# Casting loads, states on both row halves and a new instruction order in the first batches of an attention and feed-forward kernel

## The chip, the cores and the metric

The kernel runs on one core of a Trainium2 chip. The metric is device time in microseconds of one execution, the median of several runs. The engines have queues of their own and run side by side: TensorE (PE in the profile, with its weight loads as PEld), VectorE (DVE), ScalarE (ACT), Pool (POOL) and SyncE (SP, which only issues transfers here). Each engine takes its instructions in order.

## The reference

```python
B, H, S, Ns, D = 8, 8, 512, 32, 64            # x (B,H,S,D), state (B,H,Ns,D), fp32
scores  = x @ state^T / sqrt(D)               # rows: 512 tokens, over 32 states
xread   = softmax(scores) @ state
scores2 = state @ x^T / sqrt(D)               # rows: 32 states, over 512 tokens
sread   = softmax(scores2) @ x
z = concat([xread, sread], axis=2)            # (B, H, 544, D)
z = z.transpose(0, 2, 1, 3).reshape(4352, 512)
h = z @ w_in                                  # (512, 2048)
out = max(0.01 * h, h) @ w_out                # (2048, 512)
```

## The kernel before, in words

The work goes batch by batch. For the 512 token rows of a batch, `xread @ w_in` is taken as probabilities times (state @ w_in): `a_m` (L364) makes a batch's matrix M = state @ w_in in four column blocks of 512, each in two PSUM banks of 128 rows (4 heads of 32 states each), and `m_evict` (L384) casts it to bf16. `ff1` (L394) multiplies 128 columns of M with the probabilities `aT`, two matmuls of 512 columns, and ScalarE evicts the product with the leaky relu into `hT`; `ff1_pair` does two at a time. The second product, `hT` times `w_out`, is done for batch 0 in pieces of one matmul each (`piece`, L602) and for the other batches in a form with seven products instead of eight (`Batch`, L697; a unit is two matmuls of 256 columns, `Fast.unit`, L670). That form needs sums of quarters of `w_out` (`weights_sum`, L638, into the `tw` tiles) and of `hT` (`Fast.sums`, L657).

The attention of a batch: `a_scores` (L212) makes the scores of all heads in the PSUM tile "sc"; `a_shift` takes the maximum over the 32 states on VectorE, spreads it, subtracts it; `a_exp` on ScalarE; `a_probs` sums, inverts, spreads and multiplies into `aT`. `a_max2`, `a_exp2` and `a_probs2` do the softmax over tokens for the state rows, whose read (`a_sread_rows`, L335, and for the last batch `a_sread`, L320) comes later, after a transpose by DMA (`a_a2t`).

Batch 0 has an order of its own: its tokens come in four transfers, TensorE transposes them, and its ff1 is done in quads (`Quad`, L942: eight matmuls of 256 columns, over half the tokens). Ten spins of TensorE on a zero tile stand at the start (`spin`, L139).

The loads: `w_in` and `w_out` are cast to bf16 by transfers from Pool's queue, in the order of the program (L881, L903 to L912): w_in's four quarters, w_out's first quarter, batch 1's x in two halves as fp32 (`x1`), w_out's second quarter in two parts, its third, batch 2's x as fp32 (`xl`), w_out's fourth in two parts. From batch 3 on, SyncE loads x as fp32 (`load_x`, L105). The fp32 tokens are cast into `xb` by VectorE for batch 1, by ScalarE and Pool for batch 2 and by Pool after that (`cast_x`, L112). `a_xt_dma` (L199) then transposes them by DMA from SyncE's queue; batch 1's are transposed by TensorE (L1014). The states of batches 0 and 1 are transposed by matmuls (`state01`, L156), those of batches 2 to 3 and 4 to 7 by Pool's cast and a DMA transpose (`state_t`, L185). A state head lies on row half g (64 rows) for an even or odd head.

The order is written out by hand: every engine's instructions follow the program (`manual_schedule`), and PSUM tiles of one tag ("ph" and "py" with two banks each in turn, "sc" and "big" with one of two banks) are passed on when their last reader is done. Lines 976 to 1118 are the order of batches 0 and 1; the loop at L1122 does batches 2 to 7 with a list of how many units go beside each ff1 (`PACE`, and `PACE2` for batch 2). The tail (L1250 on) does the state rows.

Of the kernel before, what the change touches and what calls it, by code (L numbers as in the profile page):

```python
# [9 lines left out]
P = 128  # L10
B, H, S, D = 8, 8, 512, 64
NS = 32
# [18 lines left out]
def kernel(  # L31
# [41 lines left out]
    idle = consts.tile([P, S], BF16, name="idle")  # L73
# [6 lines left out]
    identg = consts.tile([P, 2, P - NS], BF16, name="identg")  # L80
    nc.gpsimd.memset(identg[:], 0.0)
    heads = ident[:].rearrange("p (b k v q) -> p b k v q", b=2, k=NK, v=2)
    for g in range(2):
        for u in range(2):
            nc.gpsimd.tensor_copy(
                identg[:, g, :D].rearrange("p (k v q) -> p k v q", k=NK, v=2)[:, 2 * u:2 * u + 2, g ^ u],
                heads[:, 0, 2 * u:2 * u + 2, g],
            )
        nc.gpsimd.tensor_copy(
            identg[:, g, D:].rearrange("p (k q) -> p k q", k=NK), heads[:, 1, :, g]  # L90
        )
# [11 lines left out]
    xs, xl = {}, {}  # L103

    def load_x(b, eng):  # L105
        xl[b] = xpool.tile([P, H, NT * D], FP32, name="xl", tag="xl", bufs=1)
        eng.dma_start(xl[b][:], x[b].rearrange("h (p t) d -> p h (t d)", t=NT))

    def open_xb(b):
        xs[b] = xpool.tile([P, NT, H, D], BF16, name="xb", tag="xb")  # L110

    def cast_x(b, h0, h1, copy):  # L112
        copy(  # L113
            xs[b][:, :, h0:h1].rearrange("p t h d -> p h t d"),
            xl[b][:, h0:h1].rearrange("p h (t d) -> p h t d", t=NT),
        )

# [13 lines left out]
    def load_w_out(c, parts=1):  # L131
        n = 4 // parts
        for j in range(4 * c, 4 * (c + 1), n):
            nc.gpsimd.dma_start(
                w_out_bf[:, j:j + n, :],
                moe_w_out[P * j:P * (j + n), :].rearrange("(j p) f -> p j f", p=P),
            )
# [9 lines left out]
    st1 = consts.tile([P, P], BF16, name="st1")  # L147
    groups = ((2, 4), (4, 8))
    st_t = [consts.tile([P, hi - lo, P], BF16, name=f"st_t{lo}") for lo, hi in groups]
# [4 lines left out]
    stb0 = consts.tile([P, 4, D], BF16, name="stb0")  # L154

    def state01():  # L156
        ps = psum.tile([P, 4, P - NS], FP32, name="pst0", tag="big", bufs=1)
        for r in range(4):
# [10 lines left out]
            st1[:].rearrange("p (k q r) -> p k q r", k=NK, r=4),  # L169
            ps[:, :, D:].rearrange("p r (k q) -> p k q r", q=8),  # L170
# [3 lines left out]
    stb = [consts.tile([P, hi - lo, P], BF16, name=f"stb{lo}") for lo, hi in groups]  # L174
# [10 lines left out]
    def state_t(i):  # L185
        POO(stb[i][:], stf[i][:])
        nc.sync.dma_start_transpose(st_t[i][:], stb[i][:].rearrange("p b q -> p (b q)"))

# [3 lines left out]
    def a_open(a, b):  # L194
        a.b = b
        a.xb = xs[b]
        a.xT = att.tile([P, NT, NK, P], BF16, name="xT", tag="xT")

    def a_xt_dma(a):  # L199
        nc.sync.dma_start_transpose(  # L200
            a.xT[:].rearrange("p t k q -> p (t k) q"),
            a.xb[:].rearrange("p t h d -> p (t h d)"),
        )

    def st_of(a, g, k):
        rows = slice(D * g, D * (g + 1))
# [3 lines left out]
        return t[rows, NS * k:NS * (k + 1)]  # L210

    def a_scores(a):  # L212
        sc = psum.tile([P, 2, S], FP32, name="sc", tag="sc", bufs=1)
        for k in range(NK):
            for g in range(2):
                nc.tensor.matmul(  # L216
                    sc[NS * k:NS * (k + 1), g, :],
                    lhsT=st_of(a, g, k),
                    rhs=a.xT[D * g:D * (g + 1), :, k, :],
                    start=True, stop=True,  # L220
                )
        a.sc = sc

# [37 lines left out]
    def block_probs(dst, e1, q1h, n):  # L261
        q1b = att.tile([P, n, NS], BF16, name="qb", tag="qb", bufs=1)
        nc.vector.transpose(q1b[:], q1h[:, :, None].to_broadcast([P, n, NS]))
        nc.vector.tensor_tensor(  # L264
# [4 lines left out]
    def a_shift(a, part=None):  # L269
        flat = a.sc[:].rearrange("p g c -> p (g c)")  # L270
        if part != 1:
            a.mb = block_rows(block_max(flat, NB), NB)
        if part != 0:
            a.sh = block_sub(flat, a.mb, NB)
# [4 lines left out]
    def a_probs(a, part=None):  # L279
        if part != 1:  # L280
            a.q1h = block_recip(a.e1, NB)
        if part != 0:
            a.aT = att.tile([P, 2, S], BF16, name="aT", tag="aT")
            block_probs(a.aT[:], a.e1, a.q1h, NB)

    def a_max2(a):
        m2 = att.tile([P, 2], FP32, name="mcol", tag="mcol")
        nc.vector.tensor_reduce(out=m2[:], in_=a.sc[:], axis=AX.X, op=ALU.max, negate=True)  # L288
# [3 lines left out]
    def a_exp2(a, g):  # L292
        if g == 0:
# [3 lines left out]
            out=a.e2[:, g], in_=a.sc[:, g, :], func=AF.Exp,  # L297
# [22 lines left out]
    def a_sread(a):  # L320
        ps = psum.tile([P, NK, 2, NS], FP32, name="psr", tag="big", bufs=1)
        for k in range(NK):
            for i in range(NT):
                nc.tensor.matmul(
                    ps[:, k, :, :],
                    lhsT=a.xb[:, i, 2 * k:2 * k + 2, :].rearrange("p h d -> p (h d)"),
                    rhs=a.a2T[:, :, i, NS * k:NS * (k + 1)],
                    start=(i == 0), stop=(i == NT - 1),
                )
        for g in range(2):  # L330
            nc.scalar.copy(
                sr_t[D * g:D * (g + 1), a.b], ps[D * g:D * (g + 1), :, g, :],
            )
# [1002 lines left out]
```

## Time and profile before

| | |
|---|---|
| time, median of 3 runs | 202.02 us (201.66 to 202.12) |
| profiled execution, from first to last instruction | 199.8 us, 4974 instructions |
| what the timed median lies above that span | 2.2 us |
| granted TensorE clock | 1.00 throughout |
| TensorE / VectorE / ScalarE / Pool busy | 97% / 80% / 72% / 28% |
| DMA, mean over the span | 140 GB/s, 28.01 MB |

How to read it: a timeline row has start and length in us, engine, line, operation, tiles written<-read, shapes and count; what stands in brackets is the idle time just before it and what ended it. In a group row, "busy, mean ns of one" follow the bar, then idle time and its cause. A matmul's length holds its way through the array: the distance between starts is what it costs when others follow. In the transfers' part the last figure is the median time from issue to landing.

### The profile page before, as it was taken

Reading aid. Unit: us, or ns where it says so; the run is one execution under the profiler, and the core shown is the slowest. Engines: PE = TensorE matmul, PEld = TensorE weight load, DVE = VectorE, ACT = ScalarE, POOL = GpSimd, SP = SyncE. Lnnn points to the kernel's source line nnn. Section 1 sums busy time; section 2 is a strip of 40 time slices with the busy share of each in tenths; the row PEclk is TensorE's granted clock in tenths of the full one; section 3 lists DMA queues with packets and bytes.
Section 4 is the critical chain, followed back from the end, with each engine's and each line's share of the span. In section 5 each row is a group of like instructions: output and inputs, shape, how many; then the busy total and the mean of one; then the engine's idle time right before and its main releaser. Section 6 shows DMA issues by size and latency. Waiting matters only on the chain.

```text
span 199.8 us, 4974 instructions
## 1 busy us (share of the span) xinstructions
PE 193.2 (97%) x2044; PEld 134.3 (67%) x2066; DVE 160.8 (80%) x249; ACT 143.5 (72%) x263; POOL 55.4 (28%) x82
## 2 busy tenths in 40 slices
PE   7999999999999999999999999999999999999993
PEld 2566633446676767766776677667767788799882
DVE  2676689999999989966997499879978977995622
ACT  3478748599877867877797859787878768767710
POOL 8483174690027004200320041100020024005250
PEclk9999999999999999999999999999999999999999
DMA  5999997999581993269414945290025102210035
GB/s 195 221 206 271 236 296 137 221 286 202 112 223 28 302 266 73 47 213 272 91 24 195 241 43 107 105 164 0 0 108 157 30 0 94 119 56 0 0 95 171
DMA packets 39510, 28.01 MB, mean 140 GB/s; under 512 B 25344, under 2 KB 36736, under 8 KB 39488
## 3 DMA queue, kind: packets, MB, share of 16 engines
q1 hardware_dynamic: 33712, 20.35, 40.8%
q0 software_dynamic: 4944, 6.55, 16.0%
q10 hardware_dynamic: 832, 0.79, 1.2%
q8 instruction: 16, 0.26, 0.5%
q14 instruction: 6, 0.05, 0.1%
HBM read 17.30 MB, written 8.91 MB: 131 GB/s over the span
## 4 chain that ended last, share of the span: by engine, by line
PE 96%; DVE 1%; issue 1%; ACT 1%
PE yq L679 44%; PE ph L397 20%; PE pm L376 4%; PE py L608 4%; PE pyw L608 4%; PE pf L475 3%; PE yu L679 3%; PE ph L958 3%; PE pspin L142 2%; PE pl L564 2%; PE sc L216 1%; PE psn L342 1%; PE php L958 1%; PE phw L410 1%; PE scn L826 1%
## 5 line engine op out<-in xcount | busy, mean ns | idle before, releaser
L403 ACT ACTIVATE hT<-ph 128x512 bf16<-128x512 f32 x100 | 58.5, 605 | 18.4 <-PE ph L397 11.9
L679 PEld LDWEIGHTS <-su 128*128 128x128 bf16 x480 | 45.9, 98 | 14.8 <-DVE su L668 0.8
L397 PE MATMUL ph<-aT,M 128*128 128x512 bf16 x180 | 54.4, 379 | 0.3
L679 PEld LDWEIGHTS <-hT 128*128 128x128 bf16 x336 | 32.3, 98 | 14.3 <-issue 2.5
L679 PE MATMUL yq<-tw_xf,su 128*128 128x256 bf16 x224 | 31.6, 273 | 0.3
L679 PE MATMUL yq<-w_out_bf,hT 128*128 128x256 bf16 x224 | 31.0, 273 | 0.1
L113 POOL CAST xb<-xl 128x512 bf16<-128x512 f32 (+1 forms) x24 | 13.9, 621 | 49.9 <-DMA xl<-in_x_dram 36.7
L668 DVE TENSOR_TENSOR su<-hT 128x1024 bf16<-128x1024 bf16 (+1 forms) x27 | 19.3, 718 | 6.7 <-ACT hT L403 6.7
L397 PEld LDWEIGHTS <-M 128*128 128x128 bf16 x200 | 19.5, 98 | 5.7 <-DVE aT L264 0.2
L751 POOL TENSOR_TENSOR yo<-sv,sv 128x512 f32<-128x512 f32 x7 | 9.1, 1295 | 39.2 <-ACT sv L688 19.4
L688 ACT COPY sv<-yq 128x512 f32<-128x512 f32 x28 | 16.3, 586 | 3.0 <-PE yq L679 2.5
L679 PE MATMUL yq<-w_out_bf,su 128*128 128x256 bf16 x112 | 15.3, 273 | 0.3
L679 PE MATMUL yq<-tw_x,su 128*128 128x256 bf16 x112 | 15.5, 273 | 0.0
L691 DVE TENSOR_TENSOR yo<-yq,sv 128x512 f32<-128x512 f32 x20 | 13.6, 681 | 1.5 <-PE yq L679 1.5
L679 PE MATMUL yq<-tw_x,hT 128*128 128x256 bf16 x104 | 14.5, 273 | 0.0
L390 ACT CAST M<-pm 128x1024 bf16<-128x1024 f32 x12 | 12.2, 1018 | 0.2 <-PE pm L376 0.2
L296 ACT ACTIVATE e<-sc,mcols 128x512 bf16<-128x512 f32 x16 | 11.0, 695 | 0.6 <-DVE mcols L290 0.6
L608 PEld LDWEIGHTS <-hT 128*128 128x128 bf16 x64 | 5.9, 98 | 7.0 <-issue 1.1
L668 DVE TENSOR_TENSOR su<-su,hT 128x1024 bf16<-128x1024 bf16 x14 | 9.7, 692 | 0.5
L288 DVE TENSOR_REDUCE mcol<-sc 128x2 f32<-128x1024 f32 x8 | 9.7, 1214 | 0.0
L226 DVE TRANSPOSE_TENSOR_REDUCE mrow<-sc 128x32 f32<-128x1024 f32 x7 | 8.7, 1240 | 0.5 <-PE sc L216 0.5
L668 DVE TENSOR_TENSOR su<-hT,su 128x2048 bf16<-128x2048 bf16 (+1 forms) x8 | 9.1, 1132 | 0.0
(173 smaller groups left out, 302.6 us busy)
## 6 DMA issues: line engine op xcount, KB each, us to landing
out_dram<-yo SPq DMA_DIRECT2D x12, 512.0 KB, 2.7
xl<-in_x_dram SPq DMA_DIRECT2D x5, 1024.0 KB, 6.7
w_in_bf<-in_moe_w_in_dram POOLq DMA_DIRECT2D x4, 512.0 KB, 7.8
w_out_bf<-in_moe_w_out_dram POOLq DMA_DIRECT2D x2, 512.0 KB, 12.9
x<-in_x_dram POOLq DMA_DIRECT2D x2, 512.0 KB, 11.5
w_out_bf<-in_moe_w_out_dram POOLq DMA_DIRECT2D x4, 256.0 KB, 13.7
xl<-in_x_dram POOLq DMA_DIRECT2D x1, 1024.0 KB, 16.4
out_dram<-ysb SPq DMA_DIRECT2D x4, 256.0 KB, 5.6
```

The source lines that it names most:

```text
L113: copy(xs[b][:, :, h0:h1].rearrange("p t h d -> p h t d"), xl[b][:, h0:h1].rearrange("p h (t d) -> p h t d", t=NT),)
L288: nc.vector.tensor_reduce(out=m2[:], in_=a.sc[:], axis=AX.X, op=ALU.max, negate=True)
L296: nc.scalar.activation(out=a.e2[:, g], in_=a.sc[:, g, :], func=AF.Exp, bias=a.m2s[:, g:g + 1], scale=SCALE, accum_out=a.r2[:, g:g + 1],)
L390: copy(a.M[:, :, cols], pm[:])
L397: nc.tensor.matmul(ph[:], lhsT=a.M[:, g, P * j:P * (j + 1)], rhs=a.aT[:, g, :], start=(g == 0), stop=(g == 1),)
L403: nc.scalar.activation(out=hT[:, j, :], in_=ph[:], func=AF.Prelu, alpha=0.01)
L608: nc.tensor.matmul(y.py, lhsT=hT[:, j, P * i:P * (i + 1)], rhs=w_out_bf[:, j, :], start=(j == 0), stop=(j == 15),)
L668: (eng or nc.vector).tensor_tensor(out=S[n][:, ms], in0=u[:, ms], in1=v[:, ms], op=op)
L679: nc.tensor.matmul(bank[:, i, :], lhsT=lhs[:, m, P * i:P * (i + 1)], rhs=rhs[:, m, :], start=(first and m == 0 and (i == 0 or of is not No ...
L688: copy(t[:], bank)
L691: nc.vector.tensor_tensor(out=dst, in0=bank, in1=self.sv[n][:], op=ALU.add)
L751: nc.gpsimd.tensor_tensor(out=self.yo(1)[:, :, HC:], in0=f.sv[7][:], in1=f.sv[5][:], op=ALU.add)
```

## The change

Tokens of batches 1 to 7 are loaded as bf16 by casting transfers from Pool's queue, in halves for batches 1 and 2, and there is no cast of x by an engine any more. The layout of `xb` becomes head by head, so that a transpose of 128 columns holds two of a head's four token groups: a head's tokens lie on both row halves of `xT`. So the states are put on both row halves too (`state01` and the state transposes get twice as wide, `state_cast` makes two copies), and the scores of a batch become sixteen matmuls of 256 columns instead of eight of 512. The output rows are numbered accordingly. `a_sread` of the last batch becomes 32 matmuls of 64 rows for 16 of 128. The loads from Pool go in the order w_in, x of batch 1, three quarters of w_out, x of batch 2, the last quarter. Two of `w_out`'s sums that VectorE made are Pool's. The order of everything from the second quad to the end of batch 2's stretch is new, and written out call by call: which evictions go to VectorE or ScalarE, which PSUM tile a product takes, and where the pieces, ff1 products and units stand. The loop now runs over batches 3 to 7.

```diff
-    xs, xl = {}, {}
-    def load_x(b, eng):
-        xl[b] = xpool.tile([P, H, NT * D], FP32, name="xl", tag="xl", bufs=1)
-        eng.dma_start(xl[b][:], x[b].rearrange("h (p t) d -> p h (t d)", t=NT))
+    def load_x(b, h0=0, h1=H):
+        nc.gpsimd.dma_start(
+            xs[b][:, h0:h1].rearrange("p h t d -> p h (t d)"),
+            x[b, h0:h1].rearrange("h (p t) d -> p h (t d)", t=NT),
+        )
...
-        ps = psum.tile([P, 4, P - NS], FP32, name="pst0", tag="big", bufs=1)
+        ps = psum.tile([P, 4, P], FP32, name="pst0", tag="big", bufs=1)
...
+            sc = psum.tile([P, 2, 2, S // 2], FP32, name="sc", tag="sc", bufs=1)
             for g in range(2):
+                for k in range(NK):
+                    for v in range(2):
+                        nc.tensor.matmul(
+                            sc[NS * k:NS * (k + 1), v, g, :],
+                            lhsT=st_of(a, g, k, v),
+                            rhs=a.xT[D * v:D * (v + 1), 2 * k + g, :, :],
...
     load_w_in(3)
-    load_w_out(0)
+    open_xb(2)
     for u in range(2):
-        nc.gpsimd.dma_start(
-            x1[u][:], x[1, NK * u:NK * (u + 1)].rearrange("h (p t) d -> p h (t d)", t=NT)
-        )
-    for c in range(1, 3):
-        load_w_out(c, 3 - c)
-    load_x(2, nc.gpsimd)
-    load_w_out(3, 2)
+        load_x(1, NK * u, NK * (u + 1))
+    for j in (0, 4, 8):
+        load_w_out(j, 4)
+    for u in range(2):
+        load_x(2, NK * u, NK * (u + 1))
+    load_w_out(12, 4)
...
+    def m_take(a, c, part, copy):
+        src = pm[a.b, c]
+        if part == "all":
+            copy(a.M[:, :, DM * c:DM * (c + 1)], src[:])
...
+    def p(i, js, w=None):
+        for j in js:
+            piece(0, h0, i, j // 4, bank=None if w is None else ws[0][:, w], copy=None, part=(j % 4,))
+    def state_cast(i):
+        for v in range(2):
+            POO(stb[i][:, :, :, v], stf[i][:].rearrange("p b (g d) -> p b g d", g=2))
...
+    quad(0, 4, "ph")
+    qs[0, 4].relu()
+    quad(1, 0, "big")
+    m_make(att_of[0], 2, "sc")
+    m_make(att_of[1], 1, "py")
+    quad(1, 4, "ph")
+    weights_open()
+    qs[1, 0].relu()
+    m_take(att_of[0], 2, "all", VEC)
+    qs[1, 4].relu()
+    m_make(att_of[0], 3, "sc")
+    m_take(att_of[0], 3, 1, VEC)
+    quad(0, 8, "big")
+    m_take(att_of[1], 1, 1, VEC)
+    a_scores(a0, "ph")
...
+    quad(1, 8, "py")
+    qs[1, 8].relu()
+    quad(0, 12, "big")
+    turn(1, "py")
+    quad(1, 12, "sc")
+    qs[0, 12].relu()
+    turn(0, "py")
...
+    p(0, (0, 1, 2, 3,), w=0)
+    p(1, (0, 1, 2, 3,), w=1)
+    a_scores(att_of[1])
+    m_make(att_of[1], 3, "py")
+    m_make(att_of[1], 2, "ph")
...
+    state_cast(0)
+    p(0, (4, 5, 6, 7,), w=0)
+    a_max2(att_of[1])
+    p(1, (4, 5, 6, 7,), w=1)
+    p(2, (0, 1, 2, 3,))
+    weights_sum(0, 0, 4, nc.gpsimd)
+    m_take(att_of[1], 2, 0, SCA)
+    p(0, (8, 9,), w=0)
...
+    state_turn(0)
+    a_mult(att_of[1])
+    p(2, (10, 11,))
+    p(0, (10, 11,), w=0)
+    m_make(att_of[2], 0, "sc")
...
+    ff(att_of[1], h1, 0)
+    ff(att_of[1], h1, 3)
+    a_xt_dma(att_of[2], 0, 4)
...
+    a_xt_dma(att_of[2], 4, 8)
+    open_xb(3)
+    ff(att_of[1], h1, 2)
+    a_scores(att_of[2])
...
+    weights_sum(2, 4, 8, nc.gpsimd)
+    a_less(att_of[2])
+    a_exp(att_of[2])
+    ff(att_of[1], h1, 8)
+    weights_sum(1, 4, 8)
+    p(0, (12, 13, 14, 15,), w=0)
+    a_max2(att_of[2])
+    a_a2t(att_of[0])
+    relus(att_of[1], 6)
+    load_x(3)
...
-    for b in range(2, B):
+    for b in range(3, B):
```

More of the change, by code (lines that the diff above doesn't have):

```diff
@@ L71 @@
         )
-    idle = consts.tile([P, S], BF16, name="idle")
+    idle = consts.tile([P, S], BF16, name="idle", tag="stb")
     nc.vector.memset(idle[:], 0.0)
@@ L1079, with quad, turn @@
[L1079 to L1097 removed]
+    qs, pt, ws, relu = {}, {}, {}, {}
+    def quad(u, j, tag):
+        qs[u, j] = Quad(u, j, tag)
+        qs[u, j].product()
+    def turn(u, tag):
+        pt[u] = psum.tile([P, NK, 2, P], BF16, name="pxt2", tag=tag, bufs=2 if tag in ("ph", "py") else 1)
+        for h in range(NK):
+            for v in range(2):
+                nc.tensor.transpose(
+                    pt[u][:, h, v, :],
+                    a1.xb[:, NK * u + h, 2 * v:2 * v + 2, :].rearrange("p t d -> p (t d)"), ident[:],
+                )
@@ new lines, in turned, with wide, state_turn @@
+    def turned(u, copy):
+        copy(a1.xT[:, NK * u:NK * (u + 1)], pt[u][:])
+    def wide(tag):
+        ws[0] = psum.tile([P, 2, DM], FP32, name="pyw", tag=tag, bufs=1)
+    def p(i, js, w=None):
+        for j in js:
+            piece(0, h0, i, j // 4, bank=None if w is None else ws[0][:, w], copy=None, part=(j % 4,))
+    def state_cast(i):
+        for v in range(2):
+            POO(stb[i][:, :, :, v], stf[i][:].rearrange("p b (g d) -> p b g d", g=2))
+    def state_turn(i):
+        nc.sync.dma_start_transpose(
+            st_t[i][:].rearrange("p b g q -> p (b g) q"), stb[i][:].rearrange("p b g v d -> p (b g v d)")
+        )
@@ L1177 @@
                     open_xb(b + 2)
[L1178 to L1181 removed]
+                    load_x(b + 2)
+                before.f.sums(2, 4, 8)
             elif s == 3:
```

586 lines of the change are left out of this document (339 added, 247 removed).

## The prediction

> **What bounds the kernel now.** I read the page's busy table and its chain first, then the groups by line of TensorE, then TensorE's timeline from 12 to 75 us, and last the rows of the other engines that show when transfers landed.
>
> ```profile
> PE 193.2 (97%) x2044; PEld 134.3 (67%) x2066; DVE 160.8 (80%) x249; ACT 143.5 (72%) x263; POOL 55.4 (28%) x82
> ...
> PE 96%; DVE 1%; issue 1%; ACT 1%
> ...
> L397 PEld LDWEIGHTS <-M 128*128 128x128 bf16 x200 | 19.5, 98 | 5.7 <-DVE aT L264 0.2
> ...
> L397 PE MATMUL ph<-aT,M 128*128 128x512 bf16 x180 | 54.4, 379 | 0.3
> ```
>
> A busy TensorE need not be a full one, so I check starts against starts. The 200 weight loads of L397 beside 180 matmuls say that some 20 matmuls are missing from the record: a hole of one matmul there is no idle time.
>
> ```profile
> 40.14 1.03 PE L410 MATMUL phw<-aT,M 128*128 128x512 bf16 x4
> 41.00 1.03 PE L397 MATMUL ph<-aT,M 128*128 128x512 bf16 x4
> ...
> 50.34 0.82 PE L397 MATMUL ph<-aT,M 128*128 128x512 bf16 x3
> 51.30 0.41 PE L216 MATMUL sc<-xT,st_t 64*32 64x512 bf16 x8
> ```
>
> Four matmuls of 512 columns start every 0.86 us, 0.214 each, and the rows between 12 and 70 us follow each other at that rate. The one wait that I find inside batches 1 and 2 is before 51.30: three matmuls from 50.34 are through at 50.98, 0.31 follow, of which 0.1 is the usual step to narrow tiles. So TensorE is full from 12 us to the last stores, and its work is the floor. The change takes no wide product away. It can win only 0.2 us of that wait, and switches between tile shapes; every new wait in its order costs in full.
>
> **The change part by part.** Prices of TensorE's steps:
>
> ```profile
> 15.70 0.41 PE L376 MATMUL pm<-w_in_bf,stbd 64*32 64x512 bf16 x8
> ...
> 18.07 0.41 PE L376 MATMUL pm<-w_in_bf,stbd 64*32 64x512 bf16 x8
> ...
> 18.63 1.92 PE L958 MATMUL ph<-aT,M 128*128 128x256 bf16 x16
> ...
> 22.98 0.61 PE L1014 MATMUL pxt<-ident,xb 128*128 128x128 bf16 x8
> 23.43 1.03 PE L608 MATMUL pyw<-w_out_bf,hT 128*128 128x512 bf16 x4
> ...
> 35.02 0.41 PE L376 MATMUL pm<-w_in_bf,st_t 64*32 64x512 bf16 x8
> 35.36 1.04 PE L397 MATMUL ph<-aT,M 128*128 128x512 bf16 x3
> ...
> 70.28 0.59 PE L397 MATMUL ph<-aT,M 128*128 128x512 bf16 x2
> ```
>
> A quad (8 matmuls of 256 columns) is 0.86; a piece 0.214; eight transposes 0.45. A group of narrow matmuls costs 0.34 (35.02 to 35.36) for one round of eight, 0.56 for two (18.07 to 18.63), so 0.22 more for a round, and 0.1 ahead of it.
>
> *Head.* The state transposes grow from 96 to 128 columns.
>
> ```profile
> 4.30 0.53 PE L160 MATMUL pst<-identg,stb 128*64 128x96 bf16 x8
> 4.76 1.39 PE L142 MATMUL pspin<-idle 128*128 128x512 bf16 x3
> ```
>
> 0.46 us becomes up to 0.6. The spins and the first transposes of x stand right behind it: everything 0.1 later (0 to 0.15).
>
> *Quads.* With that 0.1, quad (1,0) ends at 15.7. The products M0 column 2 and M1 column 1 now stand together: 0.56+0.1, 16.35. Quad (1,4): 17.2. M0's column 3 now goes into the bank "sc", which column 2 holds until VectorE has taken it in one cast.
>
> ```profile
> 14.16 1.22 DVE L390 CAST M<-pm 128x1024 bf16<-128x1024 f32 x1
> ...
> 16.18 1.29 DVE L974 CAST M<-pm 128x512 bf16<-128x512 f32 x2 [0.80 <-PE pm L376]
> ```
>
> The cast starts 0.48 after the product (15.70 to 16.18), so at 16.28, and ends 1.22 later at 17.5: a wait of 0.25, next step at 17.9. Then four quads, the scores of batch 0 (0.44) and twice eight transposes (0.90): 17.9+3.44+0.44+0.90, TensorE asks for the first quarter of w_out at 22.7.
>
> *The loads from Pool.* They come in order, and their rows give when the whole of each was there:
>
> ```profile
> w_out_bf<-in_moe_w_out_dram POOLq DMA_DIRECT2D x2, 512.0 KB, 12.9
> x<-in_x_dram POOLq DMA_DIRECT2D x2, 512.0 KB, 11.5
> ...
> 17.75 0.70 POOL L134 DMA_DIRECT2D w_out_bf<-in_moe_w_out_dram  x1 [1.46 <-DMA w_in_bf<-in_moe_w_in_dram]
> 20.32 0.71 POOL L134 DMA_DIRECT2D w_out_bf<-in_moe_w_out_dram  x1 [1.88 <-DMA w_out_bf<-in_moe_w_out_dram]
> ...
> 21.77 0.69 DVE L999 CAST xb<-x 128x1024 bf16<-128x1024 f32 x1 [0.59 <-DMA x<-in_x_dram]
> 23.20 0.69 DVE L999 CAST xb<-x 128x1024 bf16<-128x1024 f32 x1 [0.73 <-DMA x<-in_x_dram]
> ...
> 26.22 2.12 POOL L645 TENSOR_TENSOR tw_x<-w_out_bf 128x1024 bf16<-128x1024 bf16 x1 [5.19 <-DMA w_out_bf<-in_moe_w_out_dram]
> ...
> 31.89 1.44 POOL L113 CAST xb<-xl 128x256 bf16<-128x256 f32 x4 [1.00 <-DMA xl<-in_x_dram]
> ```
>
> The last quarter of w_in is there at 17.7, w_out's first at 20.3 (2.6 us), the halves of batch 1 at 21.75 and 23.2 (1.45 each), w_out's second at 26.2. A quarter of w_out and a half of x write the same 512 KB; w_out reads twice as much, being cast from fp32, and takes 1.8 times as long. So time goes with what is read, and a half of x that is cast still costs 1.45 (bounds 0.73, if the bytes written counted, and 2.6, a w_out transfer). The new order puts both halves ahead of w_out: its first quarter is there at 17.7+1.45+1.45+2.6=23.2 instead of 20.3, 23.3 with the head. The second stays at 26.3. The third: batch 2's x at 31.89 less its own 2 x 1.45 is 29.0, so 29.1.
>
> TensorE: 22.7, waits to 23.3 (0.6). Eight pieces (1.71) and a group of three rounds (0.88): 25.9. It asks for the second quarter and waits to 26.3 (0.4). Twelve pieces (2.57): 28.9, third quarter, waits to 29.1 (0.2). Then 26 pieces (5.56): 34.7, where batch 2's first product wants the states.
>
> *States.* Pool's row of states stays behind two sums:
>
> ```profile
> 30.49 0.40 POOL L186 CAST stb<-stf 128x256 bf16<-128x256 f32 x1
> ...
> 30.91 1.26 SPq L187 DMA_TRANSPOSE st_t<-stb  x1
> ...
> DMA to landing us min/median/max: 2.4/3.0/3.7
> ```
>
> The cast is doubled: 30.6+0.8=31.4; the transpose, twice as large, lands 3.0 to 3.7 later, 34.4 to 35.1. I take 34.7, no further wait (0 to 0.4). Batch 1's probabilities:
>
> ```profile
> 25.70 0.41 PE L216 MATMUL sc<-xT,st 64*32 64x512 bf16 x8
> ...
> 34.37 0.69 DVE L264 TENSOR_TENSOR aT<-e,qb 128x1024 bf16<-128x1024 bf16 x1
> ...
> 38.06 0.41 PE L216 MATMUL sc<-xT,st_t 64*32 64x512 bf16 x8
> ...
> 47.63 0.69 DVE L264 TENSOR_TENSOR aT<-e,qb 128x1024 bf16<-128x1024 bf16 x1
> ```
>
> 9.4 us from scores to probabilities; scores at 25.1 give 34.5, in time. So batch 1's first ff1 stands at 34.8+0.34=35.15. Before, it stood at 35.36 with 52 pieces done; the new order has 46 done. Less 6 x 0.214 that is 34.08: **1.07 behind**.
>
> *To batch 3.* The rest is the same list of products, so 35.36 to 70.28 is carried over, less the 0.2 wait at 51.30. New waits: batch 2's tokens are turned in two halves behind the states' transpose on SP (31.4+1.3, then 1.8: the second issued near 34.5; xT landed 4.3 after issue, a half sooner), for scores at 37.7: 0 to 0.3. The evictions of h stand behind batch 2's exponential on ScalarE, which waits for VectorE: two places of 0.1 to 0.2. Probabilities of batch 2: 10.3 from scores before (38.06 to 48.32), and two sums and two stores more between (0.6 each): 37.8+10.3+2.3=50.4, where 64 products of ff1, pieces and units bring TensorE to 50.0 to 50.4. I take 0.4 in all (0 to 1.2).
>
> *What costs nothing.* Casts of x on Pool, VectorE and ScalarE that go, and w_out's sums that go to Pool: none of these engines is the bound, and Pool is busy 28%. Scores as two rounds of 256 columns for one of 512: the same columns. The Trainium skill (TensorE: Matmul & The Clock Gate, Part 3: Packing small matmuls) says that weight loads overlap running matmuls only where the row group differs. By that the second round, on the same row groups, would wait out the first, some 0.2 for each of seven batches, an estimate, and the sum would be 1.2 higher. The rounds at 18.07 to 18.63, on the same row groups one after the other, cost 0.22 for 512 columns, which leaves nothing for such a wait.
>
> *Last batch.* Its state read becomes 32 narrow matmuls for 16 wide ones:
>
> ```profile
> L324 PE MATMUL psr<-a2T,xb 128*128 128x64 bf16 x16 | 0.6, 193 | 0.0
> ```
>
> Half the columns in pairs, and two switches of shape (0.1 each): between -0.1 and +0.4; I take 0.15.
>
> **Sum.** 1.07-0.2+0.4+0.15=1.4 us on the span of 199.8: 201.2. The timed runs lie 2.2 above the profiled span (202.0 against 199.8), so **203.4**.
>
> **Rivals.** (a) *Not slower: the cast halves the time of x.* At 0.73 a half, w_out is there at 21.9, 24.9 and 27.7, ahead of TensorE, and Pool's sums start 1.4 sooner, so the states are there by 33.3. TensorE then comes to the first ff1 at 33.9, held by the probabilities, 0.2 ahead of 34.08: 0.2 less 0.2 for the old wait, plus 0.55: 202.2; without any of the small waits 201.6. Against it: the two transfers of 512 KB. It decides once a half takes about 1.0 us or less.
>
> (b) *Slower: VectorE's chain of batch 2.* It meets TensorE at 50.4 with nothing to spare. Each 1 us by which it is late costs 1 us: a late xT (6.0 at worst before, against 4.3) gives +1.2 to 1.7 and 204.9. For it, by the table of windows (TensorE, its weight loads, VectorE, ScalarE, Pool, each with its count), VectorE was busy 34.24 of 35 us there before; against it, two casts and two sums leave it.
>
> ```profile
> 35.00:70.00 35.00, 34.59 (x315) 21.82 (x321) 34.24 (x52) 28.22 (x51) 13.58 (x13) 1.00 0.82 197
> ```
>
> (c) *Slower: loads from Pool.*
>
> ```profile
> xl<-in_x_dram SPq DMA_DIRECT2D x5, 1024.0 KB, 6.7
> ...
> xl<-in_x_dram POOLq DMA_DIRECT2D x1, 1024.0 KB, 16.4
> ```
>
> Batch 3's x now goes behind Pool's sums, at about 38.4, and xT takes 4.3, for scores at 52: 9.3 us to spare. At 6.7 it is hidden; at 11.5, the row of x, it costs 2.2 and gives 205.6. Against it, 16.4 and 11.5 were behind a full queue. The Trainium skill (SBUF — State Buffer, the part on DVE blocking SWDGE) says that VectorE's fast modes keep Pool from writing descriptors, which speaks for (c). The issues at 17.75 and 20.32 took 0.70 and 0.71 with VectorE at work.
>
> **How the numbers follow.** Forecast 0.66, (a) 0.16, (b) 0.12, (c) 0.06. Its own range is 202.6 to 204.2: waits from 0 to 1.2, last batch, states. Reaching to half of (a) and to (b): 202.1 to 204.9. About 0.2%, 0.4 us, is what a measurement here tells from none, so the same is 201.6 to 202.4: most of (a), 0.11. Faster needs (a) without the small waits: 0.06. Slower 0.83.
>
> **What would show it.** Right: holes in TensorE of 0.2 to 0.6 before M0's column 3 and before the first pieces of each of w_out's first three quarters, the first of them near 23.3; first ff1 near 35.2; from batch 3 on the old spacing. Wrong: the first piece at 22.7 without a hole (a), a hole before batch 2's first ff1 near 50 (b), one before batch 3's scores (c).

## The result and the profile after

The changed kernel takes **206.0 us** (205.64 to 207.61), the kernel before beside it 201.87 (201.66 to 202.12): a ratio of 1.0225 (95% interval 1.0206 to 1.0244). The forecast was 203.4 with a range from 202.1 to 204.9: the side was right, the size was not. The profiled execution has a span of 204.0 us and a time of 206.05.

The page of the changed kernel: engines, shares of the chain, and TensorE's costliest group, the only group of its matmuls on this page that shows idle time ahead of it.

```profile
PE 195.3 (96%) x2138; PEld 135.3 (66%) x2138; DVE 161.2 (79%) x249; ACT 142.9 (70%) x262; POOL 50.7 (25%) x66
...
PE 80%; DVE 10%; DMA 6%; issue 1%; ACTq 0%; POOL 0%
...
L452 PE MATMUL ph<-aT,M 128*128 128x512 bf16 x204 | 59.1, 379 | 1.8 <-DVE aT L283 1.8
```

VectorE is as busy as before (161.2 for 160.8), ScalarE and Pool are less busy (142.9 for 143.5, 50.7 for 55.4), and the time is longer. What is new stands in the chain: VectorE has 10% of it, where it had 1%, and 1.8 us of idle time before ff1 wait for `aT`, the product of batch 1's probabilities. TensorE's timeline of the changed kernel, at the places that the prediction named:

```profile
17.63 0.41 PE L416 MATMUL pm<-w_in_bf,stbd 64*32 64x512 bf16 x8 [0.34 <-DMA w_in_bf<-in_moe_w_in_dram]
...
23.02 1.90 PE L663 MATMUL pyw<-w_out_bf,hT 128*128 128x512 bf16 x8
...
25.88 1.89 PE L663 MATMUL pyw<-w_out_bf,hT 128*128 128x512 bf16 x8 [0.19 <-DMA w_out_bf<-in_moe_w_out_dram]
...
28.89 0.59 PE L663 MATMUL pyw<-w_out_bf,hT 128*128 128x512 bf16 x2 [0.26 <-DMA w_out_bf<-in_moe_w_out_dram]
...
34.76 0.41 PE L416 MATMUL pm<-w_in_bf,st_t 64*32 64x512 bf16 x8
36.95 1.04 PE L452 MATMUL ph<-aT,M 128*128 128x512 bf16 x4 [1.77 <-DVE aT L283]
...
47.98 1.02 PE L465 MATMUL phw<-aT,M 128*128 128x512 bf16 x4 [0.49 <-DVE ysb L673]
...
67.35 0.84 PE L416 MATMUL pm<-w_in_bf,st_t 64*32 64x512 bf16 x24
```

Batch 2's first product stands at 34.76, as forecast. Then the first ff1 comes at 36.95, not at 35.15. Another 0.65 is lost before 47.98, counted from the matmuls' columns. By 67.35 (batch 3's products, 63.62 before) the kernel is 3.73 behind. From there to the last batch the distance stays at 3.7. What held the two steps stands in the rows of VectorE and Pool of the changed kernel:

```profile
30.95 2.12 POOL L700 TENSOR_TENSOR tw_xf<-w_out_bf 128x1024 bf16<-128x1024 bf16 x1
31.84 1.26 DVE L271 TENSOR_SCALAR r<-r 128x32 f32<-128x32 f32 x1
...
34.22 2.12 POOL L700 TENSOR_TENSOR tw_xf<-w_out_bf 128x1024 bf16<-128x1024 bf16 x1 [1.16 <-DMA w_out_bf<-in_moe_w_out_dram]
34.80 2.09 DVE L283 TENSOR_TENSOR aT<-e,qb 128x1024 bf16<-128x1024 bf16 x1
...
44.60 2.11 POOL L700 TENSOR_TENSOR tw_x<-tw_xf,w_out_bf 128x1024 bf16<-128x1024 bf16 x1 [4.86 <-DVE tw_xf L700]
45.68 1.06 DVE L333 TENSOR_SCALAR mcols<-mcol 128x2 f32<-128x2 f32 x1
```

L271 is a step on 32 columns that takes 0.18 us elsewhere in this trace. Here it takes 1.26 and ends at 33.10, when Pool's sum ends (33.07). The product L283 takes 2.09 in place of 0.69, and ends 0.55 behind Pool's next sum (36.34). L333, a step on two columns, ends with Pool's sum at 46.7 too.

### The profile page after: what moved, and what is told of

Same layout as the page of the kernel before. It is cut to its first block, busy times and chain, and to the rows that moved or that the text cites. A ratio compares the mean times of both kernels' runs of the same rounds, so it can differ in the third digit from the quotient of the medians.

```text
span 204.0 us, 5124 instructions
## 1 busy us (share of the span) xinstructions
PE 195.3 (96%) x2138; PEld 135.3 (66%) x2138; DVE 161.2 (79%) x249; ACT 142.9 (70%) x262; POOL 50.7 (25%) x66
## 4 chain that ended last, share of the span: by engine, by line
PE 80%; DVE 10%; DMA 6%; issue 1%; ACTq 0%; POOL 0%
PE yq L734 41%; PE ph L452 20%; DMA w_in_bf<-in_moe_w_in_dram 4%; PE pm L416 3%; PE pf L530 3%; PE yu L734 3%; DMA xf<-in_x_dram 2%; PE pl L619 1%; PE php L1010 1%; DVE mrow L242 1%; DVE mrowb L250 1%; PE sc L227 1%; DVE mcol L329 1%; PE psn L382 1%; DVE aT L283 1%
## 5 line engine op out<-in xcount | busy, mean ns | idle before, releaser
L458 ACT ACTIVATE hT<-ph 128x512 bf16<-128x512 f32 x102 | 59.9, 603 | 20.0 <-PE ph L452 19.5
L452 PE MATMUL ph<-aT,M 128*128 128x512 bf16 x204 | 59.1, 379 | 1.8 <-DVE aT L283 1.8
L734 PE MATMUL yq<-w_out_bf,hT 128*128 128x256 bf16 x224 | 31.5, 273 | 0.0
L723 DVE TENSOR_TENSOR su<-hT 128x1024 bf16<-128x1024 bf16 x28 | 19.1, 681 | 7.0 <-ACT hT L458 6.8
L109 POOL DMA_DIRECT2D xb<-in_x_dram x9 | 7.6, 849 | 21.8 <-PE psn L382 20.6
L445 ACT CAST M<-pm 128x512 bf16<-128x512 f32 x16 | 9.0, 588 | 4.3 <-PE pm L416 4.2
L262 ACT ACTIVATE e<-sh 128x1024 bf16<-128x1024 f32 x7 | 7.4, 1052 | 2.6 <-DVE sh L255 2.5
L430 ACT CAST M<-pm 128x1024 bf16<-128x1024 f32 x9 | 9.1, 1014 | 0.0
```

Of the source, the lines that this page charges most:

```text
L109: nc.gpsimd.dma_start(xs[b][:, h0:h1].rearrange("p h t d -> p h (t d)"), x[b, h0:h1].rearrange("h (p t) d -> p h (t d)", t=NT),)
L430: copy(a.M[:, :, cols], pm[:])
L445: copy(a.M[:, part, DM * c:DM * (c + 1)], src[part][:] if isinstance(src, list) else src[:, part, :])
L452: nc.tensor.matmul(ph[:], lhsT=a.M[:, g, P * j:P * (j + 1)], rhs=a.aT[:, :, g, :], start=(g == 0), stop=(g == 1),)
L458: nc.scalar.activation(out=hT[:, j, :], in_=ph[:], func=AF.Prelu, alpha=0.01)
L723: (eng or nc.vector).tensor_tensor(out=S[n][:, ms], in0=u[:, ms], in1=v[:, ms], op=op)
```

## The experiments

The theory, called theory 1 below: while Pool makes a sum of `w_out`, a step of VectorE of the narrow kind (`TENSOR_SCALAR`), or one that adds or multiplies two bf16 tiles that lie in SBUF, can't begin its work until Pool's instruction is through.

**Both sums moved.** The two sums that stand beside L271 and L283 are issued behind batch 3's load.

```diff
-    weights_sum(0, 0, 4, nc.gpsimd)
...
-    weights_sum(0, 4, 8, nc.gpsimd)
...
     load_x(3)
+    weights_sum(0, 0, 4, nc.gpsimd)
+    weights_sum(0, 4, 8, nc.gpsimd)
```

> The two Pool sums of w_out that ran while VectorE made batch 1's probabilities (31.0 to 33.1 and 34.2 to 36.3 us) come after batch 3's load on Pool; all else as in the changed kernel. Theory 1 (a Pool sum holds VectorE's operations on two SBUF tiles, or fast ones on one, until it ends): the scale in L271 takes 0.2 instead of 1.26, the product into aT 0.7 instead of 2.09, batch 1's first ff1 starts near 35.1 instead of 36.95, and the time is 1.5 to 1.9 lower, about 204.3. Theory 2 (these two are slow from the new layout of aT, or from DMA writing SBUF at that time): both keep their lengths and the time stays within 0.3 of 206.0.

Measured: 203.78 us (203.75 to 204.55), ratio to the kernel before 1.0114 (1.0087 to 1.0140), span 202.0. So 2.2 of the 4.1 us are gone. Rows of this kernel's timeline:

```profile
31.77 0.18 DVE L271 TENSOR_SCALAR r<-r 128x32 f32<-128x32 f32 x1
...
33.66 0.69 DVE L283 TENSOR_TENSOR aT<-e,qb 128x1024 bf16<-128x1024 bf16 x1
...
34.66 0.41 PE L416 MATMUL pm<-w_in_bf,st_t 64*32 64x512 bf16 x8
35.00 1.04 PE L452 MATMUL ph<-aT,M 128*128 128x512 bf16 x4
...
42.64 4.19 POOL L700 TENSOR_TENSOR tw_x<-tw_xf,w_out_bf 128x1024 bf16<-128x1024 bf16 x2 [1.20 <-DVE tw_xf L700]
43.73 1.05 DVE L333 TENSOR_SCALAR mcols<-mcol 128x2 f32<-128x2 f32 x1
```

Both steps have their old lengths, and ff1 begins at 35.00, within 0.15 of the forecast. The third place, L333 beside the last pair of sums, is untouched and costs what it did.

**Only the first of the two moved.**

```diff
-    weights_sum(0, 0, 4, nc.gpsimd)
...
     load_x(3)
+    weights_sum(0, 0, 4, nc.gpsimd)
```

> Only the first of these two Pool sums is moved behind batch 3's load. Theory 1: the scale is no longer held, so the product into aT is ready to start near 33.7, before the second sum begins at 34.2 (it waits for w_out's last quarter), and is not held either: the same gain as with both moved, 1.5 to 1.9, about 204.3. If each hold cost its own time whatever the order, only 1.1 would come back, about 204.9. Theory 2: no change, 206.0.

Measured: 204.45 us (204.11 to 205.23), ratio 1.0140 (1.0113 to 1.0167), span 202.1.

```profile
33.65 0.69 DVE L283 TENSOR_TENSOR aT<-e,qb 128x1024 bf16<-128x1024 bf16 x1
...
34.22 2.12 POOL L700 TENSOR_TENSOR tw_xf<-w_out_bf 128x1024 bf16<-128x1024 bf16 x1 [2.98 <-DMA w_out_bf<-in_moe_w_out_dram]
```

The second sum stands at 34.22 as in the changed kernel, and the product takes 0.69, since it began at 33.65, ahead of it. So it is the order of the two that decides: the first hold (1.08 us at L271) had pushed the product behind the start of the second sum. The rows show this, and not the times: the first ff1 is at 35.12, 0.1 behind the kernel with both sums moved, and the spans differ by 0.1, while the medians lie 0.7 apart, for which the profiled run shows no reason.

**One sum into the kernel before.** The only thing changed in the old kernel is where one of its sums on Pool stands.

```diff
-    for m in (0, 4):
-        weights_sum(0, m, m + 4, nc.gpsimd)
+    weights_sum(0, 4, 8, nc.gpsimd)
...
         cast_x(2, h, h + 1, POO)
+    weights_sum(0, 0, 4, nc.gpsimd)
```

> The kernel before, with one thing alone changed: one of Pool's five sums of w_out (columns 0 to 3 of tw 0) is made right after Pool's casts of batch 2's tokens, at 33.3 to 35.4, instead of later. In the kernel before, VectorE's product into aT stands at 34.37 with batch 1's first ff1 right behind it at 35.36. Theory 1 (a Pool sum holds VectorE's operations on two SBUF tiles until it ends): the product lasts until 36.0, the first ff1 starts 0.6 to 0.8 later, and since TensorE is full all of that reaches the end: 202.4 to 202.7 against 201.8. Theory 2 (the stretch comes from the changed kernel's layouts or transfers): no change, 201.8.

Measured: 202.33 us (202.21 to 202.53), 0.6 above the kernel before beside it (201.72), ratio 1.0029 (1.0017 to 1.0041).

```profile
33.48 2.12 POOL L645 TENSOR_TENSOR tw_xf<-w_out_bf 128x1024 bf16<-128x1024 bf16 x1
...
34.91 1.24 DVE L264 TENSOR_TENSOR aT<-e,qb 128x1024 bf16<-128x1024 bf16 x1
...
36.20 1.04 PE L397 MATMUL ph<-aT,M 128*128 128x512 bf16 x4 [0.33 <-DVE aT L264]
```

The product takes 1.24 for 0.69, again ending 0.55 behind Pool's sum (35.60 and 36.15), and ff1 waits 0.4 for it, of the 0.6 by which the medians differ. The mechanism needs none of the rest of the change.

**Fills in place of the sums.** Both sums moved as in the first run, and four zero fills by Pool of the tiles that they write stand in their old places.

```diff
-    weights_sum(0, 0, 4, nc.gpsimd)
+    for _ in range(2):
+        nc.gpsimd.memset(tw[0][:, 0:4], 0.0)
...
-    weights_sum(0, 4, 8, nc.gpsimd)
+    for _ in range(2):
+        nc.gpsimd.memset(tw[0][:, 4:8], 0.0)
```

> As with both sums moved, but at their old places Pool fills the same tile with zeros, twice a half tile of 1024 elements a row each (overwritten later by the sums). It tells whether it is Pool being busy or Pool reading SBUF that holds VectorE. Theory 1 in its wide form (any Pool work on SBUF holds): scale and product are stretched until the fills end, time between 204.3 and 206. In its narrow form (only a Pool operation that reads SBUF): no stretch, about 204.3.

Measured: 204.57 us (204.43 to 204.68), ratio 1.0140 (1.0124 to 1.0156), span 202.2; L271 0.18, L283 0.69. The first ff1 is at 35.20, since batch 2's first product waits 0.44 for the states here; the rest of the 0.8 by which the median lies above that of both sums moved stands in no row. I first read this as "a fill holds nothing". For the product that stands. For L271 it was luck: the step came at 31.61, and a fill ended at 31.7. A later run (below) has rows that say otherwise.

**The sums on VectorE.** VectorE makes four sums, three of Pool's and one of its own, in the pause behind batch 1's product, and Pool's last pair comes behind them (the lines that leave the old places are not shown).

```diff
     m_take(att_of[2], 0, 1, VEC)
+    weights_sum(2, 4, 8)
+    weights_sum(1, 4, 8)
+    weights_sum(0, 0, 4)
+    weights_sum(0, 4, 8)
+    weights_sum(3, 4, 8, nc.gpsimd)
+    weights_sum(3, 0, 4, nc.gpsimd)
```

> VectorE makes four sums of w_out (0.61 to 0.7 each) in its idle time before batch 2's scores (37.5 to 40.1 in the changed kernel), and Pool makes only the last pair, right after them instead of at 44.6 to 48.8. Theory 1: as with both moved, and the scale in L333 at 45.7 (1.06 under a Pool sum) is short again, so the 0.66 hole of TensorE at 47.98 goes too: 2.1 to 2.7 lower, about 203.5. Theory 2: VectorE has 2.6 us more work and no relief: 206 to 207.

Measured: 208.30 us (207.63 to 208.73), ratio 1.0323 (1.0296 to 1.0349), span 206.8. Both forecasts were missed. It was meant to be free of the clash and made a worse one:

```profile
38.77 3.21 DVE L700 TENSOR_TENSOR tw_xf<-w_out_bf 128x1024 bf16<-128x1024 bf16 x2
38.93 5.03 POOL L700 TENSOR_TENSOR tw_x<-tw_xf,w_out_bf 128x1024 bf16<-128x1024 bf16 x2 [7.16 <-DVE tw_xf L700]
...
47.36 0.59 PE L452 MATMUL ph<-aT,M 128*128 128x512 bf16 x2 [2.78 <-ACT hT L458]
```

Pool's pair began while VectorE had a sum left. VectorE's two take 3.21 for 1.28, Pool's two 5.03 for 4.2: each holds the other. VectorE's chain of batch 2 is late by it, and TensorE stands for 2.9 us before 47.36. Behind that the granted clock is at half from 48.4 to 51.8, so not all of the longer span is the clash.

**No sum near a step that matters.** As above, but Pool's pair only after all of VectorE's sums, three fills on Pool for the time between, and batch 3's load issued at 33.59 (36.27 with both sums moved). Again the lines that leave their old places are not shown.

```diff
     state_cast(0)
+    for _ in range(3):
+        nc.gpsimd.memset(tw[3][:, 0:4], 0.0)
+    open_xb(3)
+    load_x(3)
...
+    weights_sum(2, 4, 8)
     m_take(att_of[2], 0, 1, VEC)
+    weights_sum(0, 0, 4)
+    weights_sum(0, 4, 8)
+    weights_sum(1, 4, 8)
+    weights_sum(3, 4, 8, nc.gpsimd)
+    weights_sum(3, 0, 4, nc.gpsimd)
```

> The changed kernel with w_out's last four sums but two on VectorE in its idle time from 34.4 to 37.8, the last two on Pool after these (37.8 to 42), zero fills on Pool from 31 to 34 in their place and batch 3's load behind the fills. No Pool sum is left beside batch 1's probabilities, beside a VectorE sum, or beside batch 2's scale of the column maximum. Theory 1: that scale takes 0.2 instead of 1.05, the two stores behind it come 0.9 sooner and the hole of TensorE at 46.03 (0.65) goes: 0.5 to 0.8 below both sums moved alone, 203.0 to 203.3. Rival (the hole is of the order of the stores, not of the hold): 203.8.

Measured: 207.95 us (207.36 to 209.78), ratio 1.0315 (1.0261 to 1.0369), span 206.0. L333 takes 0.17 and the hole at 46 to 48 is gone. But the load runs beside the transpose of batch 2's tokens. First a row of TensorE's timeline of this kernel, then one of its table of windows (window, length, busy time of TensorE, weight loads, VectorE, ScalarE, Pool, then the granted clock):

```profile
40.86 0.40 PE L227 MATMUL sc<-xT,st_t 64*32 64x256 bf16 x12 [2.85 <-DMA xT<-xb]
```

```profile
42.00:45.50 3.50, 3.50 (x11) 1.23 (x9) 3.43 (x4) 1.91 (x5) 0.62 (x1) 0.51 0.01 4
```

The scores wait 3.0 us, and shortly after that the clock is at half for 3.4 us, which costs another 1.7 (an estimate: half of the 3.4).

**The pieces in another order.** The kernel above, the state cast ahead of a sum on Pool, eight pieces that need only w_out's first quarter ahead of those of the second, and M1's column 3 later (cut here to two lines of some twelve that move).

```diff
+    p(2, (0, 1, 2, 3,))
+    p(3, (0, 1, 2, 3,))
     p(0, (4, 5, 6, 7,), w=0)
```

> As without holds, and the pieces put in an order that asks for w_out's quarters later: the first quarter for all four row blocks before the second, batch 1's column 3 of M after them, and the states' cast ahead of Pool's second sum. Theory of the prediction: the holes before the second and third quarter and before batch 2's first product go (0.27, 0.3 and 0.2), one more switch of shape costs 0.2: 0.4 to 0.6 below the one without holds, 202.4 to 202.9, 0.6 to 1.1 above the kernel before. Rival: the probabilities then bind, and less than 0.2 is won.

Measured: 204.72 us (204.55 to 205.37), ratio 1.0137 (1.0107 to 1.0167), span 202.7. TensorE has no hole any more at w_out's second and third quarter, and none at batch 2's scores. But batch 1's first ff1 is at 36.31, and VectorE's and Pool's rows of this kernel show why:

```profile
29.80 2.12 POOL L700 TENSOR_TENSOR tw_xf<-w_out_bf,tw_x 128x1024 bf16<-128x1024 bf16 x1
30.47 2.36 DVE L333 TENSOR_SCALAR mcols<-mcol 128x2 f32<-128x2 f32 x1
31.86 2.98 POOL L1117 MEMSET tw_x<- 128x1024 bf16 x3
33.12 0.74 DVE L271 TENSOR_SCALAR r<-r 128x32 f32<-128x32 f32 x1
```

L333 ends at 32.83, with the first of the three fills and not with the sum before it; L271 ends at 33.86, with the second. So a fill holds these narrow steps after all. The product of the probabilities ends late by it, and the forecast of 202.4 to 202.9 was missed.

**w_out sooner.** The first run's kernel, with x of batch 1's second half loaded last; the scores of batch 1's heads 4 to 7 use heads 0 to 3 instead.

```diff
-        load_x(1, NK * u, NK * (u + 1))
+    load_x(1, 0, NK)
...
     load_w_out(12, 4)
+    load_x(1, NK, H)
```

> The changed kernel with both Pool sums moved behind batch 3's load, and the second half of batch 1's x loaded last, behind all of w_out; left out of the computation: the scores of batch 1's heads 4 to 7 take the tokens of heads 0 to 3. It tells what it costs that w_out comes behind x. Theory of the prediction (w_out's arrival holds the pieces): the holes of TensorE at 22.9, 25.8 and 28.8 (0.23, 0.37 and 0.39, the second with 0.1 for the switch of shape) go, since w_out comes 1.3 sooner; the states, which wait for Pool's sums of w_out, come sooner as well: 0.5 to 0.9 less than with the sums moved alone, 202.9 to 203.3. Rival (the holes hide what the states or the probabilities would cost anyway): they move to the products behind, less than 0.3 is won.

Measured: 205.18 us (204.59 to 205.53), ratio 1.0160 (1.0129 to 1.0191), span 203.5. The holes at the first three quarters, 0.9 us in the first run, are gone. The stretch from M0's column 3 to the first ff1 takes 17.0 us (19.50 to 36.51) against 17.5 in the first run (17.51 to 35.00). So 0.5 is won there and not 0.9, since TensorE waits 0.47 for `aT` at the end of it. That wait is a hold again, in Pool's and VectorE's rows of this kernel:

```profile
33.78 2.12 POOL L700 TENSOR_TENSOR tw_x<-w_out_bf 128x1024 bf16<-128x1024 bf16 x1 [2.01 <-DMA w_out_bf<-in_moe_w_out_dram]
...
35.18 1.27 DVE L283 TENSOR_TENSOR aT<-e,qb 128x1024 bf16<-128x1024 bf16 x1
```

The product takes 1.27 for 0.69 and ends 0.55 behind the sum (35.90 and 36.45). At its usual length it would have ended at 35.87, ahead of the 36.04 at which TensorE could have begun ff1. So by these rows the holes at w_out cost their full length here; no run without this hold shows it.

The head is 2.0 us later for another reason. First a row of TensorE's timeline of this kernel, then one of its table of windows:

```profile
11.07 0.47 PE L416 MATMUL pm<-w_in_bf,stbd 64*32 64x512 bf16 x8 [1.49 <-DMA w_in_bf<-in_moe_w_in_dram]
```

```profile
11.30:14.70 3.40, 3.40 (x82) 2.07 (x75) 1.89 (x4) 1.36 (x3) 2.71 (x4) 0.50 1.24 207
```

In the profiled run TensorE waited 1.5 us for w_in, and behind that its clock was at half for 3.4 us. Why is not settled; so this run tells of the stretch and not of the whole.

**The load at its old time, and the fills shifted.** The kernel with no sum near, with six fills for three; and the same with a half fill ahead of them.

```diff
-    for _ in range(3):
+    nc.gpsimd.memset(tw[3][:, 0:2], 0.0)
+    for _ in range(6):
         nc.gpsimd.memset(tw[3][:, 0:4], 0.0)
```

(The first of the two is without the added line of the half fill.)

> Six fills by Pool (a stand-in for time, they write a sum's tile before its sum) in place of three, so that batch 3's load is issued near 36.5 us as it was with the two sums moved, instead of 33.6; four of w_out's sums stay on VectorE and no Pool sum runs from 42.5 on. Theory 1 (VectorE's two narrow steps and its product were late because Pool's sums held them, and what undid the last try was the early load that ran beside batch 2's transpose): the transposed tokens are there in time, no hole of 3 us at 40.9, no half clock after it, the narrow step L333 takes 0.2 us, no hole of 0.65 near 46: the profiled span is 202.0 less 0.65, 201.35, and the time 203.1 (202.8 to 203.5). Rival: four sums more on VectorE between 34 and 38.5 make its chain of batch 2 late by themselves, whatever the load does: the scores' hole stays, or a hole near 46 to 48 comes back, and the time is 203.8 or more.

> As the kernel before it in this set, with one fill of half size ahead of the six: the ends of the fills are 0.5 us later, so that VectorE's narrow step L271 (near 31.6) and its product L283 (near 33.5) fall into the middle of a fill instead of onto the end of one. If a fill holds what VectorE does with one operand in the fast form but not a sum of two bf16 operands, as two rows of an earlier try suggest (2.36 and 0.74 us for a step of 0.18, both ended with a fill): L271 takes 0.5 to 0.8 us and ends with a fill, the product still takes 0.69. If fills hold nothing: 0.18 and 0.69. If they hold both: 0.5 to 0.8 and 1.0 to 1.4. The time is that of the kernel before it within 0.3 us in any of these, since the product still ends ahead of the states at 34.7, or up to 0.5 more if both are held.

Measured: 204.46 us (203.84 to 204.82), ratio 1.0126 (1.0107 to 1.0144), span 202.1; and 204.60 (203.43 to 205.44), ratio 1.0131 (1.0096 to 1.0167), span 201.5. Timeline rows, first of the one, then of the other:

```profile
43.89 0.17 DVE L333 TENSOR_SCALAR mcols<-mcol 128x2 f32<-128x2 f32 x1
...
46.14 1.03 PE L465 MATMUL phw<-aT,M 128*128 128x512 bf16 x4
```

```profile
31.43 6.00 POOL L1121 MEMSET tw_x<- 128x1024 bf16 x6
31.83 0.60 DVE L271 TENSOR_SCALAR r<-r 128x32 f32<-128x32 f32 x1
...
34.13 0.69 DVE L283 TENSOR_TENSOR aT<-e,qb 128x1024 bf16<-128x1024 bf16 x1
```

In the stretch theory 1 holds: no 3 us hole at batch 2's scores, none before 46.14 (0.65 in the first run), and from batch 2's first product to batch 3's scores both take 17.61 us where the first run took 18.21: 0.60 less. Both kernels also take a sum of VectorE's own (0.6) out of the chain ahead of L333, so the 0.60 is not the hold's alone. That the hold alone is enough is worked out from the first run's rows: without its 0.88 the two stores would end at 45.10 and not at 45.98, ahead of the 45.38 at which TensorE is through with what stands before. The forecast of the time, 203.1, was missed in both: the heads came 0.1 to 0.7 later than in the first run (batch 2's first product at 35.37 and 34.76 against 34.66, with longer waits for w_out in the former), and the timed runs differ among themselves by 1.0 and 2.0 us (two of the second kernel's four had a granted clock of 0.99 in the mean, at 205.21 and 205.44; the other two, at 1.00, took 203.43 and 203.98). So the 0.6 is shown in the stretch, in two kernels, and not in the median. The shifted fills settle the other point: L271 takes 0.60 and ends with a fill (32.43; in the other kernel it takes 0.41 and ends with one too), while the product begins in the middle of a fill (33.43 to 34.43) and takes 0.69.

**Waits for w_out filled.**

```diff
-    m_make(att_of[2], 0, "sc")
     h1 = hpool.tile([P, 16, S], BF16, name="hT", tag="hT")
     y1 = Batch(1, h1)
     ff(att_of[1], h1, 0)
+    m_make(att_of[2], 0, "sc")
```

(With the pieces' other order, six fills, and the state cast at its old place.)

> The first kernel of this set, with 8 pieces that need only w_out's first quarter moved ahead of those of its second, M1's column 3 made behind them (so TensorE does not come early to the second and third quarter), and batch 1's first ff1 ahead of batch 2's first product, so that it waits only for the probabilities (there from 34.3 on) and not for the states. Theory (the 1.07 by which the prediction put the first ff1 behind is waits for w_out, and these can be filled with work that is there): holes at 25.8 and 28.8 gone, first ff1 near 34.4 instead of 35.0, 0.6 less than the first kernel of the set: 202.5 (202.2 to 202.9). Rival (the waits only change their place, as when the loads were put in another order: then VectorE's chain is the bound): first ff1 at 35.0 and the time within 0.2 of the first kernel of the set, or above it.

Measured: 204.88 us (204.21 to 206.34), ratio 1.0156 (1.0128 to 1.0184), span 202.8. The forecast of 202.5 was wrong, and the rival right on the time:

```profile
31.59 1.25 DVE L267 TRANSPOSE_TENSOR_REDUCE r<-e 128x32 f32<-128x1024 bf16 x1 [1.07 <-ACT e L262]
...
35.54 0.60 PE L452 MATMUL ph<-aT,M 128*128 128x512 bf16 x2 [1.23 <-DVE aT L283]
```

The holes at w_out are gone, and TensorE comes to ff1 1.4 early. The evictions that were moved ahead stand before batch 1's exponential on ScalarE, VectorE waits 1.07 for it, and `aT` ends at 35.48 (34.35 in the first run). So the waits for w_out can be filled, and this order lost the gain by putting the chain of the probabilities back; what an order would win that leaves the chain alone is open.

## Why the prediction was right on the side and wrong in size

*The step that failed* is "What costs nothing", and in it the reason "none of these engines is the bound, and Pool is busy 28%". By it the prediction put at nothing what Pool's sums of `w_out` cost, and looked at neither what a sum does to VectorE nor where the new order puts the sums. In the changed kernel it is not the two sums that newly go to Pool that hold. The three that hold were Pool's before, as Pool's rows of the kernel before show:

```profile
36.55 2.13 POOL L645 TENSOR_TENSOR tw_x<-tw_xf,w_out_bf 128x1024 bf16<-128x1024 bf16 x1 [3.22 <-DVE tw_xf L645]
38.63 4.21 POOL L645 TENSOR_TENSOR tw_xf<-w_out_bf 128x1024 bf16<-128x1024 bf16 x2
```

There all three stood behind the product of batch 1's probabilities (34.37) and ahead of VectorE's next narrow step (43.66). The new order puts the latter two at 30.95 and 34.22, where they hold L271 and L283 for 1.1 and 1.4 us on the chain of batch 1's probabilities, and the first at 44.60, beside L333. Moving the two takes 1.95 off the first ff1 (36.95 to 35.00, 0.1 of it an earlier head) and 2.2 off the time. The third holds L333 for 0.9, which puts two stores late, and 0.6 of that reaches TensorE. Together that is some 2.5 us, none of which the sum had; with it, 203.4 would have been 205.9. That 206.0 was measured is this close partly by luck: the other terms are off by tenths in both directions, and the median lies 2.0 above the span instead of 2.2.

The trace of before had it to be read. These are its VectorE and Pool rows at a place where nothing waited for them:

```profile
61.27 1.07 POOL L186 CAST stb<-stf 128x512 bf16<-128x512 f32 x1
62.30 1.26 POOL L751 TENSOR_TENSOR yo<-sv,sv 128x512 f32<-128x512 f32 x1
63.05 0.55 DVE L255 TENSOR_SCALAR r<-r 128x32 f32<-128x32 f32 x1
```

The same step takes 0.19 at 32.48; here it ends at 63.60, with Pool's instruction (63.56). The Trainium skill (SBUF — State Buffer, "Who interferes with whom") says so as a rule of the port pair that VectorE and GpSimd (Pool) share: the pair is an exclusive lock that is held for a whole instruction, `tensor_scalar` can enter a mode that takes it, and an operation with two SBUF inputs clashes with it only against a GpSimd operation that reads SBUF. The runs agree in each part: 1.26 and 0.60 for 0.18 beside a sum and a fill, 2.09 for 0.69 beside a sum, 0.69 beside a fill. The prediction drew on this page of the Trainium skill for Pool's transfers alone, in rival (c), and did not weigh this rule.

*Point by point.* The first ff1 was put at 35.15; without the two holds it is at 35.00, so **"1.07 behind" was right to 0.15**. Its parts are less so: the waits of 0.6, 0.4 and 0.2 for w_out's quarters are 0.20, 0.26 (0.35 with the step between shapes) and 0.43, since TensorE asked for the first 0.1 later and it came 0.3 sooner (a half of x takes 1.33 us by the transfers' records, not 1.45). So that the total came out is partly luck. The head's 0.1 did not come (15.70 to 15.69). The hole before M0's column 3 is 0.51 with the 0.1 of the step to narrow tiles, 0.4 instead of 0.25: here w_in's last quarter came last, while in other kernels of the set it is 0.32 and VectorE's cast is named, as forecast. Batch 2's first product is at 34.76, forecast 34.8, 0.27 behind the last piece, of which 0.1 is the step between shapes and the rest a wait for the states, inside the bounds.

*To batch 3*: -0.2+0.4 was forecast, 0.86 came, of it 0.6 the hold; without it 0.2 to 0.3. *Steady state*: the scores of batch 4 stand 3.73 later and those of batch 7 3.68, so the new layout with its scores of sixteen matmuls costs nothing there. The scores of batch 4 take 0.23 to the next product, before and after, so the waiting between rounds on the same row groups, by which the prediction's rule from the Trainium skill (TensorE: Matmul & The Clock Gate, Part 3: Packing small matmuls) would have added 0.2 a batch, does not show; for the seven batches named there that would have been 1.4, not 1.2. *Last batch*: 0.15 was forecast; the state read costs 0.24 more with the step between shapes ahead of it, an old wait of 0.13 goes and a new one of 0.15 comes. Another 0.27 lies behind the last products. The sum of the rows is 0.92 to the first ff1 without the two holds, 1.95 for these, 0.86 to batch 3, 0.2 from there to the last product and 0.27 behind it: 4.2, the two spans' difference.

*Rivals.* (a) decided at 1.0 us a half; it is 1.33, and the holes at w_out's quarters are there. (c) did not come: no hole at batch 3's scores. (b) was half right on the place: a hole at 47.98 for want of VectorE. Its reason, that VectorE has too much to do (34.24 of 35 us), was wrong: with three of Pool's sums on VectorE and none on Pool beside L333, that hole went away.

No version tried beats the kernel before.

## What to carry to other kernels

Before work goes to an idle engine, or to another time on it, look at what its instructions do to the engine beside it: search the trace for one short step that is sometimes three to ten times as long as usual, and see with whose instruction it ends. Such a hold costs what is left of the other's instruction, so what counts is which of the two starts first, and a hold early in a chain can push a later step into the next one. And a wait that is seen on TensorE is only worth its length if the next chain that is due is not late: here 0.9 us of waits went and 0.5 was won, because another sum on Pool then held the probabilities, and two other tries put that chain back themselves.

## What the runs showed of the hardware beside this

- A VectorE step that is held through one instruction of Pool can lose to the next one too: 2.36 us for 0.17, through the rest of a sum and a whole fill.
- Not all of VectorE's steps are held. In the changed kernel a transpose, two reductions and a step with one operand in PSUM begin inside Pool's sums and keep their lengths: L250 1.25 (at 26.61), L267 1.23 (47.85), L329 1.22 (29.04) and L255 1.22 (27.89).
- The hold goes both ways: two sums of VectorE against two of Pool took 3.21 and 5.03 us instead of 1.28 and 4.2.
- After TensorE holes of 2.9 and 3.0 us the granted clock fell to half for 3.4 us, 1.1 and 1.2 us behind the end of the hole (0.51 from 42.0 to 45.5 in the second case). In one run it fell for as long 0.2 us behind a hole of 1.5 us (the one that ends at 11.07). After the changed kernel's hole of 1.8 us it did not fall in the profiled run. So the length of the hole alone does not decide it; what does is open.
- A load of 512 KB cast to bf16 that was issued at 33.6 put the tokens' transpose by DMA so late that the scores waited 3 us; with the same kernel, three fills more and the load at 37.6 they did not wait. The second half of the tokens landed 7.3 us after the issue of its transpose in the first case and 3.3 at most in the other.
